# A memory-bound decode step on one core: from a planned tile program to one looped program per engine, with a running maximum

## The chip, the core and the metric

The kernel runs on one core of a Trainium2 chip. TensorE (PE) multiplies matrices, VectorE (DVE) and ScalarE (ACT) work on vectors, GpSimd (POOL) sets up a constant, and SyncE (SP) issues the transfers between the chip's main memory and the on-chip buffers; 16 DMA engines carry them out. Each engine follows its own instruction stream and waits for the others by semaphores. The metric is the device time of one execution in microseconds (us); lower is better.

## The reference

One token (batch 1, length 1, width 1024) goes through two branches that a gate mixes. Everything is float32.

```python
x = A_x                                             # (1, 1, 1024)
g = sigmoid((x * gate_w).sum(-1, keepdims=True))
# branch a: attention, 32 query heads, 4 key/value heads, 65536 cached positions, head width 128
q = (x @ wq) as 32 heads                            # wq 1024 x 4096; 8 query heads share a key/value head
p = softmax(q . k * 128 ** -0.5)                    # k_cache, v_cache: (1, 4, 65536, 128)
a = (p @ v) as one row @ wo                         # wo 4096 x 1024
# branch b: gated feed-forward on the one token, which is always the one routed
y = (silu(x @ w_gate) * (x @ w_up)) @ w_down        # 1024 x 3584, 1024 x 3584, 3584 x 1024
b = x + y * sigmoid(x @ w_r)
out = g * a + (1 - g) * b
```

The key and value caches are 134 MB each and the weights 78 MB; each is used once.

## The kernel before, in words

The arrays are laid out on the host so that every load is 128 rows, one for each partition, with up to 64 KB in a row. `stream` is a pool of two buffers of 64 KB a partition (`bufs=2`); `room` takes the next one, `load` fills it from SP's queue (line 70). All large loads share these two in turn: a load can be issued when PE has finished with the buffer two loads back. The order of the work is that of the program text, and the framework that it is written in places the waits.

For each of the four head groups (one key/value head and its eight query heads):

- `queries` multiplies x with the group's part of wq and spreads the eight queries into `qp` as stationary operands of 32 columns (L130, L138).
- Eight chunks of 8192 positions, two to a load of keys (8.39 MB). `score_chunk` does 16 products of 512 columns in four column groups of the array, which run beside each other (L149); in the profile each float32 product is two instructions. ACT copies the scores out of PSUM into a buffer of their own (L153), and DVE takes their row maximum (L154). The scores of all eight chunks are kept.
- `neg_max`, once per group: the maximum over all chunks and rows goes through a small product (L164) and becomes the exponential's bias `nb` (L169).
- Eight chunks again, two to a load of values: `value_chunk` exponentiates a chunk (L173), DVE transposes it in blocks of 32 (L175), and PE does 16 products that add into `acc` over all chunks (L178).
- `project` divides by the sums and multiplies with the group's part of wo into `att` (L191, L193, L201). wo of the group and wq of the next come in one load.

Into the key and value loops `load_eighth` (L237) puts 16 transfers of 64 KB: each brings eight rows of two of the 28 blocks of w_down, into a buffer `early` of their own. Four are issued in each head group, two between key loads and two between value loads:

```python
    eighths = [slice(32 * q + r, 32 * q + r + 29, 4) for r in range(4) for q in range(4)]

    def load_eighth():
        rows = eighths.pop()
        a = begins[w0 + b_early]
        nc.sync.dma_start(early[rows], tail[rows, a : a + 2 * D].rearrange("p (b n) -> p b n", b=2))
```

After the groups comes the tail. `load_rest` (L218) brings the last group's wo, then w_gate, w_up and w_down in pieces, through the same two buffers. `up_proj` makes the gate and up rows (L276), brings them into columns (L281, L284), and the product is `hp` (L295). The down-projection takes 4 products of 256 columns a block into `y` (L312); the last block is cut in two pieces of columns with loads of their own (L319). DVE joins y, att and x (L324), and SP stores the result (L325). At the end of the program the framework has all engines meet and clears the semaphores (L355).

Of the kernel before, what the change touches and what calls it, by code (L numbers as in the profile page):

```python
# [2 lines left out]

# [6 lines left out]
F32 = mybir.dt.float32  # L10
AF = mybir.ActivationFunctionType
ALU = mybir.AluOpType
# [7 lines left out]
SK = 65536  # L20
F = 3584
CH = 8192
NCH = SK // CH
NL = NCH // 2
NM = CH // 512
NB = CH // P
W = 16384
KB = D // P
NQ = D // 4
FB = F // P  # L30
FQ = FB // 4
SCALE = DH ** -0.5


@with_exitstack
def gated_mix_kernel(ctx: ExitStack, tc: tile.TileContext, x, vecs, k_t, v, wq0, wo_wq, tail, out):

    nc = tc.nc
    const = ctx.enter_context(tc.tile_pool(name="const", bufs=1))
    stream = ctx.enter_context(tc.tile_pool(name="stream", bufs=2))
    scores = ctx.enter_context(tc.tile_pool(name="scores", bufs=NCH + 2))
    work = ctx.enter_context(tc.tile_pool(name="work", bufs=2))
    ps_s = ctx.enter_context(tc.tile_pool(name="ps_s", bufs=2, space=bass.MemoryType.PSUM))
    ps_o = ctx.enter_context(tc.tile_pool(name="ps_o", bufs=2, space=bass.MemoryType.PSUM))
    ps_1 = ctx.enter_context(tc.tile_pool(name="ps_1", bufs=1, space=bass.MemoryType.PSUM))  # L60

    def room(*shape):
        t = stream.tile([P, W], F32, name="st", tag="st")
        names = " ".join("abcd"[: len(shape)])
        t = t[:, : math.prod(shape)]
        return t.rearrange(f"p ({names}) -> p {names}", **dict(zip("abcd", shape))) if len(shape) > 1 else t

    def load(src, *shape):
        t = room(*shape)
        nc.sync.dma_start(t, src)  # L70
        return t


    xk = const.tile([P, 3, KB], F32, name="xk")
    nc.scalar.dma_start(xk, vecs)
    x_row = const.tile([P, NQ], F32, name="x_row")
    nc.vector.memset(x_row, 0.0)

    wq_t = load(wq0, KB, HG * DH)

    ident = const.tile([P, P], F32, name="ident")
    make_identity(nc, ident)
    ones = const.tile([P, P], F32, name="ones")
    nc.vector.memset(ones, 1.0)

    sel = const.tile([P, 32], F32, name="sel")
    nc.vector.tensor_reduce(sel, ident.rearrange("p (j q) -> p q j", q=32), AX.X, ALU.add)
    sel8 = const.tile([P, HG], F32, name="sel8")
    nc.vector.tensor_reduce(sel8, ident.rearrange("p (a h) -> p h a", h=HG), AX.X, ALU.add)
    nsel = const.tile([P, HG], F32, name="nsel")  # L90
    nc.vector.tensor_scalar_mul(nsel, sel8, -SCALE)
    sel4 = const.tile([P, 4], F32, name="sel4")
    nc.vector.tensor_copy(sel4, ident.rearrange("p (j h) -> p j h", h=32)[:, :, 0])


    xp = const.tile([P, KB, 32], F32, name="xp")
    nc.vector.memset(xp, 0.0)
    nc.vector.tensor_copy(xp[:, :, 0], xk[:, 0, :])

    qp = const.tile([P, 2, 4, 32], F32, name="qp")  # L100
    nc.vector.memset(qp, 0.0)
    op = const.tile([P, HG, 32], F32, name="op")
    nc.vector.memset(op, 0.0)
    hp = const.tile([P, FB, 32], F32, name="hp")
    nc.vector.memset(hp, 0.0)


    dots = const.tile([P, 2, KB], F32, name="dots")
    for i in range(2):
        nc.vector.tensor_mul(dots[:, i, :], xk[:, 0, :], xk[:, 1 + i, :])  # L110
    dsum = const.tile([P, 2], F32, name="dsum")
    nc.vector.tensor_reduce(dsum, dots, AX.X, ALU.add)  # L112
    ps = ps_1.tile([P, P], F32, name="ps_m", tag="m")
    nc.tensor.matmul(ps[:, :2], ones, dsum, start=True, stop=True)  # L114
    sig = const.tile([P, 2], F32, name="sig")
    nc.scalar.activation(sig, ps[:, :2], AF.Exp, scale=-1.0)
    nc.vector.tensor_scalar_add(sig, sig, 1.0)
    nc.vector.reciprocal(sig, sig)
    gate = sig[:, 0:1]
    rest = const.tile([P, 2], F32, name="rest")  # L120

    nc.vector.tensor_scalar(rest[:, 0:1], gate, -1.0, 1.0, op0=ALU.mult, op1=ALU.add)
    nc.vector.tensor_mul(rest[:, 1:2], rest[:, 0:1], sig[:, 1:2])
    att = ps_1.tile([P, NQ], F32, name="att", tag="att")

    def queries(g, wq_t):
        ps = ps_s.tile([P, 512], F32, name="ps_q", tag="s")
        for k in range(KB):
            for j in range(4):
                nc.tensor.matmul(  # L130
                    ps[32 * j : 32 * j + 32, :NQ], xp[:, k, :], wq_t[:, k, j * NQ : (j + 1) * NQ],
                    start=(k == 0), stop=(k == KB - 1),
                )
        q_sb = work.tile([P, NQ], F32, name="q_sb")
        nc.vector.tensor_copy(q_sb, ps[:, :NQ])  # L135
        pt = ps_1.tile([P, P], F32, name="ps_m", tag="m")
        for e in range(2):
            nc.tensor.matmul(pt[:, 4 * e : 4 * e + 4], q_sb[:, e * DH : (e + 1) * DH], sel4, start=True, stop=True)  # L138
# [220 lines left out]
```

## Time and profile before

| what | value |
|---|---|
| median of 3 runs | 819.33 us (819.08 to 819.88) |
| span of the profiled execution, first to last instruction | 817.2 us |
| profiled execution's own device time | not given; the median is 2.1 us above the span |
| instructions | 6762, of them 3142 products and 3142 weight loads on PE |
| bytes moved | 346.47 MB, 424 GB/s over the span |
| mean granted TensorE clock | 0.730 |

An engine's share of busy time is an average; which work sets the end is read from the stretches and from the chain of waits. "PE" counts products and "PEld" weight loads, which run beside them. In the table by stretches each row has the stretch, its length, the busy time and the number of instructions of each engine, the granted clock of PE (1.00 is full), the busy share of the DMA engines (it can be a little over 1, as overlapping packets count twice) and the rate. In the chain a row is: start, length, what ran.

### The profile page before, as it was taken

The numbers are of one execution on the slowest core, as the hardware profiler recorded it, in microseconds if no ns is written. First come the engines' busy times: TensorE is split into PE (matmuls) and PEld (weight loads), VectorE is DVE, ScalarE is ACT, GpSimd is POOL, SyncE is SP. The second block draws the span as 40 slices with busy tenths as digits, with TensorE's granted clock in tenths as the row PEclk, the third lists the DMA queues.
The fourth block names the chain that finished last, engine by engine and source line by source line (L and its number), as shares of the span: only waits on it lengthen the run. The fifth ranks groups of instructions, "written<-read, shape, count | busy, mean of one in ns | idle before, by whom it ended". The sixth has DMA issues, their size and how long they took to land.

```text
span 817.2 us, 6762 instructions
## 1 busy us (share of the span) xinstructions
PE 396.5 (49%) x3142; PEld 129.6 (16%) x3142; DVE 64.4 (8%) x149; ACT 45.6 (6%) x101; POOL 0.7 (0%) x6
## 2 busy tenths in 40 slices
PE   2445454444444444454544555455444544444657
PEld 1111111112111111112111111122111111121214
DVE  2000020000000200000000200000000200000000
ACT  0000020000000200000000300000000300000000
POOL 0000000000000000000000000000000000000000
PEclk9667776776677667766677767777777677776768
DMA  9999999999999999999999999999999999999996
GB/s 411 411 456 415 420 453 420 434 430 440 424 427 427 420 433 432 433 434 431 423 427 427 427 430 440 427 440 424 421 433 424 433 427 442 424 403 438 413 412 268
DMA packets 7355, 346.47 MB, mean 424 GB/s; under 512 B 1048, under 2 KB 1184, under 8 KB 1440
## 3 DMA queue, kind: packets, MB, share of 16 engines
q1 hardware_dynamic: 7184, 346.04, 98.8%
q8 instruction: 24, 0.39, 0.2%
q10 hardware_dynamic: 144, 0.01, 0.0%
q14 instruction: 3, 0.02, 0.0%
HBM read 346.05 MB, written 0.00 MB: 423 GB/s over the span
## 4 chain that ended last, share of the span: by engine, by line
DMA 72%; PE 25%; ACT 1%; issue 0%; DVE 0%; SPq 0%; ACTq 0%
DMA st<-in_k_t 30%; DMA st<-in_v 26%; DMA st<-in_tail 10%; PE ps_s L149 9%; PE acc L178 9%; DMA st<-in_wo_wq 7%; PE att L201 2%; PE ps_f L276 2%; PE y L312 2%; PE ps_q L130 1%; ACT s L173 1%; PE ps_t L284 0%; ACT row L281 0%; PE y L319 0%; DVE mx L154 0%
## 5 line engine op out<-in xcount | busy, mean ns | idle before, releaser
L149 PE MATMUL ps_s<-st,qp 128*32 128x512 f32 x1024 | 145.6, 732 | 168.1 <-DMA st<-in_k_t 168.1
L178 PE MATMUL acc<-st,pt 128*32 128x512 f32 x1024 | 146.7, 737 | 126.1 <-DMA st<-in_v 126.1
L149 PEld LDWEIGHTS ps_s<-st,qp 128*32 128x32 f32 x1024 | 40.1, 131 | 270.3 <-issue 270.3
L178 PEld LDWEIGHTS acc<-st,pt 128*32 128x32 f32 x1024 | 37.7, 132 | 231.6 <-issue 188.1
L153 ACT ACTIVATE s<-ps_s 128x512 f32<-128x512 f32 x32 | 19.1, 597 | 575.0 <-PE ps_s L149 575.0
L276 PE MATMUL ps_f<-st,xp 128*32 128x448 f32 x256 | 34.6, 703 | 31.3 <-DMA st<-in_tail 31.3
L154 DVE TENSOR_REDUCE mx<-s 128x1 f32<-128x512 f32 x32 | 22.0, 686 | 295.7 <-ACT s L153 295.7
L201 PE MATMUL att<-st,op 128*32 128x256 f32 x256 | 25.2, 579 | 33.3 <-DMA st<-in_wo_wq 25.6
L175 DVE STREAM_TRANSPOSE pt<-s 128x512 f32<-128x512 f32 x32 | 22.7, 712 | 174.7 <-PE acc L178 170.9
L173 ACT ACTIVATE s<-s,nb 128x512 f32<-128x512 f32 x32 | 22.6, 707 | 10.7 <-DVE nb L169 10.7
L201 PEld LDWEIGHTS att<-st,op 128*32 128x32 f32 x256 | 13.1, 165 | 43.9 <-issue 43.3
L276 PEld LDWEIGHTS ps_f<-st,xp 128*32 128x32 f32 x256 | 9.4, 138 | 55.2 <-DMA st<-in_tail 34.5
L191 PE MATMUL ps_m<-sel,lb 128*128 128x8 f32 x8 | 2.3, 357 | 28.9 <-DVE lb L187 28.9
L130 PE MATMUL ps_q<-st,xp 128*32 128x256 f32 x256 | 16.2, 410 | 0.0
L312 PE MATMUL y<-st,hp 128*32 128x256 f32 x200 | 11.5, 392 | 0.0
L281 ACT ACTIVATE row<-ps_f 128x896 f32<-128x896 f32 x2 | 1.8, 917 | 151.6 <-PE ps_f L276 151.6
L130 PEld LDWEIGHTS ps_q<-st,xp 128*32 128x32 f32 x256 | 9.0, 118 | 6.2 <-issue 1.8
L189 DVE COPY o_sb<-acc 128x512 f32<-128x512 f32 x4 | 2.8, 692 | 90.6 <-PE acc L178 90.6
L114 PE MATMUL ps_m<-dsum,ones 128*128 128x2 f32 x2 | 0.6, 364 | 13.8 <-DVE dsum L112 13.8
L312 PEld LDWEIGHTS y<-st,hp 128*32 128x32 f32 x200 | 6.3, 115 | 5.4 <-issue 1.1
L191 PEld LDWEIGHTS ps_m<-sel,lb 128*128 128x128 f32 x8 | 2.0, 310 | 29.8 <-issue 29.8
L135 DVE COPY q_sb<-ps_q 128x256 f32<-128x256 f32 x4 | 1.7, 425 | 57.1 <-PE ps_q L130 57.1
(57 smaller groups left out, 51.3 us busy)
## 6 DMA issues: line engine op xcount, KB each, us to landing
st<-in_tail SPq DMA_DIRECT2D x3, 7168.0 KB, 25.1
st<-in_tail SPq DMA_DIRECT2D x2, 7680.0 KB
st<-in_wq SPq DMA_DIRECT2D x1, 4096.0 KB
st<-in_tail SPq DMA_DIRECT2D x1, 4096.0 KB
st<-in_tail SPq DMA_DIRECT2D x1, 2048.0 KB
st<-in_tail SPq DMA_DIRECT2D x2, 1024.0 KB
early<-in_tail SPq DMA_DIRECT2D x16, 64.0 KB
st<-in_tail SPq DMA_DIRECT2D x1, 512.0 KB
```

The costliest lines, as they stand in the source:

```text
L130: nc.tensor.matmul(ps[32 * j : 32 * j + 32, :NQ], xp[:, k, :], wq_t[:, k, j * NQ : (j + 1) * NQ], start=(k == 0), stop=(k == KB - 1),)
L149: nc.tensor.matmul(ps[32 * j : 32 * j + 32, :], qp[:, g % 2, s, :], kt[:, s, j, :], start=(s == 0), stop=(s == 3))
L153: nc.scalar.activation(t, ps, AF.Copy)
L154: nc.vector.tensor_reduce(mx[:, c : c + 1], t, AX.X, ALU.max)
L173: nc.scalar.activation(t, t, AF.Exp, bias=nb, scale=SCALE, accum_out=sums[:, c : c + 1])
L175: nc.vector.transpose(pt, t)
L178: nc.tensor.matmul(acc[32 * j : 32 * j + 32, :], pt[:, 32 * m : 32 * m + 32], vt[:, 4 * m : 4 * m + 4, :], start=(c == 0 and m < 4), stop= ...
L189: nc.vector.tensor_copy(o_sb, acc.rearrange("p (s d) -> p s d", s=4))
L191: nc.tensor.matmul(ps[:, :HG], lb, sel8, start=True, stop=True)
L201: nc.tensor.matmul(att[32 * j : 32 * j + 32, :], op[:, h, :], wo_t[:, h, j * NQ : (j + 1) * NQ], start=(g == 0 and h == 0), stop=(g == G - ...
L276: nc.tensor.matmul(ps[32 * j : 32 * j + 32, e, :n], xp[:, k, :], rest_of[first + k][:, at : at + n], start=(k == 0), stop=(k == KB - 1),)
L312: nc.tensor.matmul(y[32 * j : 32 * j + 32, :], hp[:, b, :], rest_of[w0 + b][:, j * NQ : (j + 1) * NQ], start=(b == order[0]), stop=False,)
```

## The change

The kernel is rewritten without the framework. Each engine has a program of its own with hand-written semaphore waits; PE's loops over groups and over block pairs are loops on the chip, and the other engines' programs are written out.

- There are three buffers of 64 KB a partition: `kb` for keys, `vb` for values, `wb` for weights. SP's queue alternates key and value loads. A key load waits until PE has done the scores of the key block before (`k_done`), a value load until PE has done the value products of the value block before (`v_done`). A weight load waits for the queries that use the other half of `wb` (`q_rows`).
- A block is one load, 16384 positions: 32 products into a PSUM tile S of 1024 columns. DVE takes the maximum straight from S; there is no copy to the on-chip buffer.
- The softmax keeps a running bound: after each key block the bound `nb` is updated, ACT exponentiates S at once, and DVE multiplies the running sums `l1` and `acc` with `alpha = exp(nd)` before it adds the new block. So scores and values of a block follow each other, 16 times in all.
- Output, gate and down products of 256 columns become products of 512; the sums of two column groups are joined at the end by a product with a selection matrix (`selj`). x @ wq, wo and w_down all run through `tiles`.
- The transfers of 64 KB are gone. x is loaded at the start from ACT's queue. In the tail the loads are: last wo, half of w_gate, half of w_gate, half of w_up, half of w_up, 16 blocks of w_down, then 8, 2, 1 and the last block in two pieces.
- There is no meeting of the engines at the end: SP waits for the store, and the program ends.

The core of the diff (removed lines stand in the kernel above):

```diff
+    def load(dst, src, sem, n=0):
+        if n:
+            sp.wait_ge(pe.sem, n)
+        sp.dma_start(dst, src).then_inc(sem, 16)
+
+    load(wb[:, W // 2 :], wq0, s_w)
+    for g in range(G):
+        for i in range(NL):
+            b = (g, i - 1) if i else (g - 1, NL - 1)
+            load(kb, k_t[g, i], s_k, k_done(*b) if b[0] >= 0 else 0)
+            load(vb, v_t[g, i], s_v, v_done(*b) if b[0] >= 0 else 0)
+        if g < G - 1:
+            load(wb, wo_wq[g], s_w, q_rows(g))
+        else:
+            load(wb[:, : W // 2], tail[:, : W // 2], s_w, q_rows(g))
...
+    for dst, n, sem, after in (
+        (kb, half, s_k, k_done(G - 1, NL - 1)),
+        (vb, half, s_v, v_done(G - 1, NL - 1)),
+        (wb, half, s_w, att_done(G - 1)),
+        (kb, half, s_k, FFN + 1),
+        (vb, W, s_v, FFN + 2),
+    ):
+        load(dst[:, :n], tail[:, at : at + n], sem, after)
+        at += n
+    parts = [8 * D, 2 * D, D] + [4 * (c1 - c0) for c0, c1 in PIECES]
+    for k, n in enumerate(parts):
+        to = at - down - W
+        load(wb[:, to : to + n], tail[:, at : at + n], s_part[k], 0 if k else FFN + 4)
+        at += n
...
+    with p.Fori(0, G):
...
+        with p.Fori(0, NL):
+            landed(s_k)
+            kv = kb.rearrange("p (c s j n) -> p c s j n", c=2, s=4, j=4)
+            for c in range(2):
+                for s in range(4):
+                    for j in range(4):
+                        ins = mm(
+                            S[32 * j : 32 * j + 32, 512 * c : 512 * c + 512], qp[:, 32 * s : 32 * s + 32], kv[:, c, s, j, :],
+                            s == 0, s == 3,
+                        )
+            pe(ins)
+            event()
+            pe(mm(M[:, :P], ones, md))
+            event()
+            landed(s_v)
+            vv = vb.rearrange("p (c m n) -> p c m n", c=2, n=512)
+            for c in range(2):
+                for m in range(16):
+                    j = m % 4
+                    ins = mm(
+                        A[32 * j : 32 * j + 32, :], pt[:, 512 * c + 32 * m : 512 * c + 32 * m + 32], vv[:, c, m, :],
+                        c == 0 and m < 4, c == 1 and m >= 12,
+                    )
+            pe(ins)
...
+        for i in range(NL):
+            dve.wait(pe, k_done(g, i))
+            d(v.tensor_reduce(m1, S, AX.X, ALU.max))
+            dve.own()
+            tell_pe(v.tensor_scalar_mul(md, ident, m1))
+            dve.wait(pe, m_done(g, i))
+            d(v.tensor_reduce(mh, M[:, :P].rearrange("p (a h) -> p h a", h=HG), AX.X, ALU.max))
+            dve.own()
+            d(v.tensor_mul(mh, mh, nsel))
+            dve.own()
+            d(v.tensor_reduce(nbi, mh, AX.X, ALU.add))
+            dve.own()
+            d(v.tensor_tensor(nb, nbi, nb0, ALU.min))
+            dve.own()
+            d(v.tensor_tensor(nd, nb, nb0, ALU.subtract))
+            dve.own()
+            d(v.tensor_copy(nb0, nb))
+            act.wait(dve)
+            act(a.activation(alpha, nd, AF.Exp))
+            act(a.activation(t, S, AF.Exp, bias=nb, scale=SCALE, accum_out=sums))
+            dve.wait(act)
+            d(v.scalar_tensor_tensor(l1, l1, alpha, sums, op0=ALU.mult, op1=ALU.add))
+            tell_pe(v.transpose(pt, t))
+            dve.wait(pe, v_done(g, i))
+            d(v.scalar_tensor_tensor(acc, acc, alpha, A, op0=ALU.mult, op1=ALU.add))
...
+    landed(s_v)
+    d1 = vb.rearrange("p (b n) -> p b n", n=D)
+    tiles(T, [hp[:, b, :] for b in range(16)], d1, False, False)
+    p.wait_ge(s_part[0], 16)
+    d2 = wb[:, : 8 * D].rearrange("p (b n) -> p b n", n=D)
+    join_ready = pe(tiles(T, [hp[:, 16 + b, :] for b in range(8)], d2, False, True))
+    later = wb[:, 8 * D : 11 * D].rearrange("p (b j n) -> p b j n", b=3, j=4)
+    for b in range(3):
+        if b != 1:
+            p.wait_ge(s_part[1 + b // 2], 16)
+        for j in range(4):
+            for (c0, c1), o in zip(PIECES, y):
+                mm(o[32 * j : 32 * j + 32, :], hp[:, JOIN + b, :], later[:, b, j, c0:c1], b == 0, False)
+        if b == 1:
+            event()
+            for j in range(4):
+                for (c0, c1), o in zip(PIECES, y):
+                    c = (j % 2) * 256
+                    mm(o[32 * j : 32 * j + 32, :], selj[:, j // 2, :], join[:, c + c0 : c + c1], False, False)
...
+    sp.wait_ge(dve.sem, dve.n)
+    sp.dma_start(out.rearrange("(j n) -> j n", j=4), fin[::32, :]).then_inc(s_out, 16)
+    sp.wait_ge(s_out, 16)
```

`event()` makes PE wait for one signal of `tell_pe`; `landed(sem)` makes it wait for a load; `pe(ins)` counts the steps that other engines wait for. `own()` makes DVE wait for its last step.

More of the change, by code (lines that the diff above doesn't have):

```diff
@@ L1 @@
[L1 to L5 removed]
+import concourse.bacc as bacc
 from concourse import mybir
[L7 to L8 removed]
 F32 = mybir.dt.float32
@@ new lines, in gated_mix, with tell_pe @@
+        pe(ins)
+        at += 4 * n
+    y_done = [pe.n - 1, pe.n]
+    pool(gp.memset(ident, 0.0))
+    pool.own()
+    pool(
+        gp.affine_select(
+            out=ident, in_=ident, compare_op=ALU.not_equal, fill=1.0, base=0, pattern=[[-1, P]], channel_multiplier=1
+        )
+    )
+    def tell_pe(ins):
+        ins.then_inc(to_pe, 1)
+    d = dve
+    d(v.memset(x_row, 0.0))
+    act.wait(dve)
+    a.dma_start(x_row[::32, :], x4).then_inc(s_x4, 16)
+    d(v.memset(join, 0.0))
+    d(v.memset(ones, 1.0))
@@ new lines, in gated_mix @@
+    d(v.tensor_copy(selj[:, :, 0], selq))
+    v.wait_ge(s_x, 16)
+    d(v.tensor_copy(xp[:, :, 0], xk[:, 0, :]))
+    for i in range(2):
+        d(v.tensor_mul(dots[:, i, :], xk[:, 0, :], xk[:, 1 + i, :]))
+    dve.own()
+    tell_pe(v.tensor_reduce(dsum, dots, AX.X, ALU.add))
+    act.wait(pe, 1)
+    act(a.activation(sig, M[:, :2], AF.Exp, scale=-1.0))
+    dve.wait(act)
+    d(v.tensor_scalar_add(sig, sig, 1.0))
+    dve.own()
+    d(v.reciprocal(sig, sig))
+    dve.own()
+    d(v.tensor_scalar(rest[:, 0:1], sig[:, 0:1], -1.0, 1.0, op0=ALU.mult, op1=ALU.add))
@@ new lines, in gated_mix @@
+    for u in range(2):
+        act.wait(pe, FFN + 3 * u + 2)
+        if u:
+            act.wait(dve)
+        a.activation(
+            row.rearrange("p (e n) -> p e n", e=2), R.rearrange("p (e n) -> p e n", e=2)[:, :, :FR], AF.Copy
+        ).then_inc(to_pe, 1)
+        cols = FFN + 3 * u + 3
+        if u == 0:
+            act.wait(pe, cols)
+            act(a.activation(hid, S[:, :FB], AF.Exp, scale=-1.0))
+            dve.wait(act)
+            d(v.tensor_scalar_add(hid, hid, 1.0))
+            dve.own()
+            d(v.reciprocal(hid, hid))
+            dve.own()
+            d(v.tensor_mul(hid, S[:, :FB], hid))
+            dve.own()
+            d(v.tensor_scalar_mul(hid, hid, rest[:, 1:2]))
+        else:
+            dve.own()
+            dve.wait(pe, cols)
+            tell_pe(
+                v.tensor_mul(
+                    hp[:, :, 0].rearrange("p (j m) -> p m j", j=4), S[:, :FB].rearrange("p (m j) -> p m j", j=4),
+                    hid.rearrange("p (m j) -> p m j", j=4),
+                )
+            )
```

448 lines of the change are left out of this document (185 added, 263 removed).

## The prediction

> **What bounds the kernel now.** I read the page from the top: busy times, the slices, the DMA queues.
>
> ```profile
> span 817.2 us, 6762 instructions
> PE 396.5 (49%) x3142; PEld 129.6 (16%) x3142; DVE 64.4 (8%) x149; ACT 45.6 (6%) x101; POOL 0.7 (0%) x6
> DMA  9999999999999999999999999999999999999996
> DMA packets 7355, 346.47 MB, mean 424 GB/s; under 512 B 1048, under 2 KB 1184, under 8 KB 1440
> q1 hardware_dynamic: 7184, 346.04, 98.8%
> q8 instruction: 24, 0.39, 0.2%
> ```
>
> No engine is over half busy; the 16 DMA engines are over 90% busy in all slices but the last. SP's queue (q1) moves 346.04 MB, and the new kernel must move the same weights and caches. So the question is only at what rate those bytes flow, and what lies ahead of the first and behind the last of them. Next I cut the span into stretches: per head group one from before the second key load lands to after the fourth (the key stretch) and one with the value loads and what follows (the value stretch); then the feed-forward tail.
>
> ```profile
> core 0: us, PE busy (x) PEld busy (x) DVE busy (x) ACT busy (x) POOL busy (x), PEclk, DMA share, GB/s
> 0.00:5.00 5.00, 0.00 (x0) 0.00 (x0) 2.03 (x6) 1.28 (x1) 0.70 (x6) 1.00 0.69 243
> 45.00:95.00 50.00, 20.38 (x140) 5.77 (x144) 2.75 (x4) 2.39 (x4) 0.00 (x0) 0.67 0.99 424
> 95.00:220.00 125.00, 65.44 (x520) 21.42 (x512) 11.13 (x26) 7.70 (x20) 0.00 (x0) 0.72 1.01 434
> 220.00:272.00 52.00, 20.53 (x144) 5.78 (x148) 3.43 (x5) 2.83 (x5) 0.00 (x0) 0.72 0.99 420
> 272.00:398.00 126.00, 65.74 (x516) 21.74 (x508) 11.13 (x26) 7.93 (x20) 0.00 (x0) 0.71 1.01 434
> 398.00:450.00 52.00, 19.86 (x144) 5.69 (x148) 3.43 (x5) 2.59 (x5) 0.00 (x0) 0.72 1.01 426
> 450.00:575.00 125.00, 64.43 (x516) 21.18 (x508) 11.83 (x27) 8.13 (x20) 0.00 (x0) 0.74 1.00 430
> 575.00:628.00 53.00, 22.26 (x148) 6.16 (x152) 2.74 (x4) 2.39 (x4) 0.00 (x0) 0.72 1.00 424
> 628.00:705.00 77.00, 34.88 (x252) 9.52 (x248) 8.56 (x17) 6.94 (x18) 0.00 (x0) 0.72 1.00 431
> 705.00:785.00 80.00, 45.52 (x370) 15.98 (x362) 1.77 (x6) 1.11 (x2) 0.00 (x0) 0.75 1.00 423
> 785.00:805.00 20.00, 12.30 (x114) 5.68 (x118) 0.21 (x1) 0.92 (x1) 0.00 (x0) 0.66 0.95 407
> 805.00:813.00 8.00, 8.00 (x155) 4.32 (x144) 0.84 (x2) 0.00 (x0) 0.00 (x0) 1.00 0.70 259
> ```
>
> The last column is what to read. The four value stretches (95, 272, 450, 628) have a weighted mean of 432.4 GB/s; I take it as the rate of an undisturbed queue. Against it the four key stretches lose (432.4-424)/432.4 x 50 = 1.0, then 1.5, 0.8 and 1.0 us: **4.3 us**. The feed-forward stretches lose 1.7 + 1.2 = **2.9 us**, the last eight microseconds **3.2 us**, the first five **2.2 us**. Check: 346.47 MB at 432.4 GB/s are 801.3 us, and with the 12.6 lost 813.9; the stream ends at about 813, where the last stretch was cut. So the stream explains the span, and about 10 us of it can be attacked.
>
> Last the chain, for how far ahead the loads are issued, and for the end.
>
> ```profile
> 32.46 9.95 PE ps_s L149 x64
> 42.43 30.30 DMA st<-in_k_t
> 72.86 8.53 PE ps_s L149 x64
> ...
> 634.02 0.70 DVE mx L154
> ...
> 634.94 0.30 DVE md L162
> ...
> 635.28 0.59 PE ps_m L164 x2
> ...
> 636.42 0.17 DVE nb L169
> ...
> 766.25 25.06 DMA st<-in_tail
> ...
> 799.98 13.23 PE y L312 x216
> ...
> 813.22 0.71 PE y L319 x16
> ...
> 813.95 0.48 DVE fin L324
> ```
>
> A load is issued when PE leaves the buffer before last (42.43) and lands 30.30 us later; its own 8.39 MB take 19.4 us at 432.4 GB/s, so 10.9 us of the load ahead were still to come: that is the margin before the queue runs dry.
>
> **The change, part by part.**
>
> *The buffers.* Two rotating buffers become three fixed ones (keys, values, weights), and key and value blocks alternate. The next key load waits for the scores of the key block before it, while one value load is in flight; the next value load waits for the value matmuls, while one key load is in flight. The margin is as now: PE needs 8.5 to 9.95 us of the 19.4 us that the other load takes, and 9.5 to 10.9 stay. At the ends of head groups it grows, since the weight buffer is free long before. I cost the new order at 0; its cover is that margin. If it goes, each block costs what is over.
>
> *The running maximum.* It puts the softmax between the scores and values of each pair, 16 times instead of four. The steps, with the chain's rows and these two:
>
> ```profile
> L175 DVE STREAM_TRANSPOSE pt<-s 128x512 f32<-128x512 f32 x32 | 22.7, 712 | 174.7 <-PE acc L178 170.9
> L173 ACT ACTIVATE s<-s,nb 128x512 f32<-128x512 f32 x32 | 22.6, 707 | 10.7 <-DVE nb L169 10.7
> ```
>
> Maximum over 1024 columns at most 2 x 0.70 = 1.4; from the product with the maximum to the negated bound 636.59 - 634.94 = 1.65; three more one-column DVE steps at 0.2 = 0.6; two exponentials, at most 0.2 + 2 x 0.71 = 1.6; one more DVE step 0.2; transpose at most 1.4; hops 0.3. Sum 7.2 us. Scores end 8.5 to 9.95 us after the key block has landed, so the transposed weights stand at 15.7 to 17.2, before the value block lands at 19.4. Hidden, with 2.2 us to spare, and behind that the 9.5 us margin of the queue. The value rescale (one DVE step over 128x512, about the 0.70 of a row above) lies beside the next load. Cost 0.
>
> *Removed: 16 small transfers* (load_eighth, 64 KB each, SP's queue). Both halves of a head group have two of them, yet only the key stretches lose rate. By the code the key ones fill rows 64 to 127 and the value ones rows 0 to 63; whether that is why is open, and so is whether the key stretches' loss is theirs at all. Bounds: 0 and 4.3. Beside them SP issues only the large loads in either kind of stretch, so I take 4.0. Their 1 MB does not vanish; it goes into the tail's loads at the same rate.
>
> The Trainium skill (DMA: Bandwidth & Descriptors, Measured) gives 0.95 us of DMA time for a 64 KB transfer. By that, estimated, 16 of them hold the queue for 15 us against 2.4 us for the same bytes in a large load, so 12.8 us would go, and the sum would be about 803.5. The value stretches, at full rate with half of these transfers in them, do not agree.
>
> *The start.* The 4 KB of x move from SP's queue in the tail to ACT's queue at the start, behind a DVE memset and the vecs load.
>
> ```profile
> xk<-in_vecs ACTq DMA_DIRECT2D x1, 12.0 KB, 12.4
> ```
>
> DVE waits for both before it copies the first queries, and PE for DVE. If x too lands 12.4 us after its issue, that is at about 14 us; the first scores start at 32.46, on the first key load. Covered by these 18 us, as are the four zeroing products that PE gets: 0.
>
> *The tail's loads* are issued farther ahead. Now the up-projection's load goes out at 766.25 and lands after 25.06 us, 18.2 of them its own 7.86 MB at 432.4: only 6.9 us ahead of it, issue latency included. The last three go out at the very end:
>
> ```profile
> SPq L218 <- PE y L312: 14.6, 1, 14.6
> 805.95 1.28 SPq L218 DMA_DIRECT2D st<-in_tail  x3
> ```
>
> In the new kernel the last five loads wait only for the first half of the up-projection, some 34 us before the end of the stream. Of the 2.9 us I take back 1.5 (bounds 0 and 2.9: loads of other row lengths follow one another there still), of the 3.2 us 0.8 (bounds 0 and 2.2; DMA engines that end at different times remain).
>
> *Code.* Loops replace 6284 PE instructions; q8's 0.39 MB are 0.9 us of stream. I take 0.4 back (bounds -0.3, if every iteration fetches anew, and 0.8).
>
> The stream thus ends 4.0 + 1.5 + 0.8 + 0.4 = **6.7 us** earlier (bounds about 0 and 10).
>
> *The end on PE.* The last 16 KB a row (2.1 MB, 4.9 us) come after the eight-block load (9.7 us), that after the sixteen-block one. With E the end of the stream, the sixteen blocks land at E-14.6 and cost 64 PE instructions of 512 columns, 8.5 to 9.95 us by the score rows: E-4.6 at the latest. The eight then cost, by
>
> ```profile
> L312 PE MATMUL y<-st,hp 128*32 128x256 f32 x200 | 11.5, 392 | 0.0
> ```
>
> 0.0575 us an instruction of 256 columns, 64 x 0.0575 = 3.7: E-0.9. Behind them stand three blocks, the join of the 512-wide sums and the last pieces, five sets of 16 short instructions. L319's set took 0.71 with its drain; I take 0.5 each and 0.2 once: E+1.8 (bounds E+1.0 and E+2.7). The copy of the sums for the join (0.7) runs beside the first two sets. Now PE ends at 813.93, E+0.9. So **+0.9 us**, less 0.1 because the last DVE step has 64 columns: **+0.8**.
>
> *The end barrier.*
>
> ```profile
> L355 SPq EVENT_SEMAPHORE  x7: 17/28/1067, 815.1 to 817.1; - x7
> ```
>
> SP's wait for the output ends at 815.1 + 1.07 = 816.2; the 1.0 us after it is barrier and clearing of semaphores. It goes: **-1.0**. The opening barrier belongs to the program's frame and I leave it.
>
> Sum: 817.2 - 6.7 + 0.8 - 1.0 = 810.3 us of span. The profiled execution's own time is not given; the median, 819.33, stands 2.1 above its span, and I keep that: **812.4 us**, 0.85% less.
>
> **The rivals.**
>
> *A. The loss of the key stretches is not the small transfers', and the tail keeps its gaps.* For it: the cause is read from a coincidence of stretches. Then only barrier, code and about 1 us of late issue go: 819.3 - 1.0 - 0.4 - 1.0 + 0.8 = **817.7 us**. Against it: four key stretches out of four, none of the value ones.
>
> *B. More is gained than costed*: the tail runs at the full rate (another 1.4), the engines end together (another 1.4), the code goes wholly (0.4), and something of the 2.1 us around the span goes with barriers and small transfers (up to 2): **807 to 809 us**. The 0.95 us a transfer of the Trainium skill (above) would be its far end. Against it: nothing in the new tail makes DMA engines wait for one another.
>
> *C. Slower: loop-backs drain the queue.* If PE, on jumping back, stands still for its code, the next scores or values start late. One fetch of 16 KB took 0.2% x 817.2 x 16 / 24 = 1.1 us by q8's row; the loop body is some 270 instructions, 17 KB, so two fetches, say twice 1.1 and twice a wait behind one 64 KB packet (65536 bytes at 1/16 of 432.4 GB/s, 2.4 us): 7 us. It decides from about 10 us on, when a value load's release comes after the key load ahead of it has landed; above that each microsecond costs 15 to 16. At 11 us: 812.4 + 15 = **827 us**. Against it: 7 is under 10, and the jump falls where PE waits for a load.
> The Trainium skill (Runtime: NRT & Kernel Launch, Instruction fetch mechanics) says that a taken branch out of the current window must fetch its target before execution goes on; no run here shows it yet, since the kernel before has no loop.
>
> *D. Slower: the clock in the tail.* PE waits before the sixteen-block load. If the granted clock stayed at half there, where the 805 to 813 row has 1.00, down-projection and join would take twice the full-clock time: (192 x 0.0575 + 2.7) x 2 = 27.5 us from E-14.6, ending at E+12.9 instead of E+1.8: about **823 us**. It decides from E+9. Against it: score bursts of 64 instructions after a wait took 9.95, not 14.7.
>
> **How the numbers follow.** Forecast 0.70, its own range 810 to 815 (about 2.5 us either way, from the bounds of the rate terms and of PE's end). A 0.13, B 0.10, C 0.04, D 0.03. 0.2%, about what a measurement can tell here from no change, is 1.6 us: the edge is 817.7, where A lies, and half of A counts as same, with a little of the forecast's upper side: faster 0.84, same 0.09, slower 0.07. The range 808.0 to 817.5 takes in the forecast, half of A and half of B; outside stay C, D, the other halves and the forecast's edges, about 0.2.
>
> **What would show it.** Right: the key stretches at 430 GB/s or more; last bytes at about 806; PE ending 1 to 3 us after the last landing; span's end within 0.2 us of the output's landing; no DMA slice under 9 but the last. Wrong, and how: key stretches still at 424 (A); value matmuls starting on the transposed weights and not on the value load's landing (the softmax is longer than 7.2 us); gaps in the stream at each jump back (C); a clock of 0.5 after the sixteen-block load (D).

## The result and the profile after

The changed kernel takes 806.84 us (median of four runs, 806.70 to 807.21) against 819.61 for the kernel before beside it (819.08 to 820.05): a ratio of 0.985, 95% interval 0.9836 to 0.9864. The gain is 12.8 us where 6.9 were forecast. The direction and the places were right; the size was not, and the time lies 1.2 us below the low end of the range.

The page of the changed kernel, its lines that answer to those shown of before:

```profile
span 805.3 us, 6266 instructions
PE 397.9 (49%) x2878; PEld 124.0 (15%) x2878; DVE 91.9 (11%) x243; ACT 24.2 (3%) x53; POOL 0.7 (0%) x6
DMA  9999999999999999999999999999999999999997
DMA packets 6935, 346.15 MB, mean 430 GB/s; under 512 B 904, under 2 KB 1040, under 8 KB 1296
q1 hardware_dynamic: 6776, 346.04, 99.3%
q8 instruction: 5, 0.08, 0.0%
```

SP's queue still moves 346.04 MB, and no engine is near to being the bound; DVE is busier by 27.5 us for the running maximum, at no cost to the kernel (the row of DVE further down). What moved is the rate, 424 to 430 GB/s over the span, and the last digit of the slices, 6 to 7. The line to keep in mind is the last: q8, the code, went from 24 packets to 5. The stream by stretches, in the columns of the prediction's table, and the last microseconds one by one:

```profile
core 0: us, PE busy (x) PEld busy (x) DVE busy (x) ACT busy (x) POOL busy (x), PEclk, DMA share, GB/s
45.00:95.00 50.00, 22.71 (x146) 6.31 (x150) 6.10 (x13) 1.95 (x5) 0.00 (x0) 0.67 1.01 439
95.00:220.00 125.00, 63.64 (x460) 19.59 (x452) 14.57 (x37) 2.59 (x6) 0.00 (x0) 0.75 0.99 429
220.00:272.00 52.00, 24.48 (x170) 7.05 (x174) 6.62 (x17) 2.59 (x6) 0.00 (x0) 0.71 1.02 441
272.00:398.00 126.00, 61.33 (x440) 18.78 (x431) 16.47 (x42) 3.89 (x9) 0.00 (x0) 0.74 1.00 434
5.00:705.00 700.00, 342.75 (x2402) 103.48 (x2406) 86.25 (x221) 20.91 (x49) 0.00 (x0) 0.74 1.00 435
705.00:785.00 80.00, 39.51 (x304) 14.44 (x296) 1.14 (x5) 2.03 (x3) 0.00 (x0) 0.69 0.99 429
799.00:800.00 1.00, 1.00 (x12) 0.26 (x8) 0.00 (x0) 0.00 (x0) 0.00 (x0) 1.00 0.97 380
800.00:801.00 1.00, 1.00 (x28) 0.63 (x24) 0.27 (x1) 0.00 (x0) 0.00 (x0) 1.00 0.41 154
801.00:802.00 1.00, 1.00 (x40) 0.89 (x32) 0.42 (x1) 0.00 (x0) 0.00 (x0) 1.00 0.11 39
```

The same view of the kernel before, the long stretch and its last microseconds:

```profile
5.00:705.00 700.00, 329.83 (x2498) 103.35 (x2502) 59.10 (x133) 42.27 (x97) 0.00 (x0) 0.72 1.00 430
809.00:810.00 1.00, 1.00 (x24) 0.54 (x20) 0.00 (x0) 0.00 (x0) 0.00 (x0) 1.00 0.98 372
810.00:811.00 1.00, 1.00 (x24) 0.60 (x20) 0.00 (x0) 0.00 (x0) 0.00 (x0) 1.00 0.55 208
811.00:812.00 1.00, 1.00 (x28) 0.52 (x21) 0.00 (x0) 0.00 (x0) 0.00 (x0) 1.00 0.24 92
812.00:813.00 1.00, 1.00 (x24) 0.44 (x16) 0.00 (x0) 0.00 (x0) 0.00 (x0) 1.00 0.12 44
```

Two things are to be seen. Over the 700 us of attention the queue runs at 435 against 430 GB/s: 5/430 x 700 = 8.1 us (give or take one and a half, since both rates are rounded). These rates count a packet whole where it starts, and sixteen packets of 64 KB are 1.05 MB, 21 GB/s of a stretch of 50 us. Spread over the time that they took, the packets of the two traces give 434.0 against 430.0 GB/s, 6.5 us. Key and value stretches are no more told apart, since the loads alternate; the 429 of one stretch and the 441 of the next belong to one steady stream, 433.9 to 434.3 when spread. And the stream now ends sharply. A DMA share of 0.55, then 0.24, then 0.12 means that fewer and fewer of the 16 DMA engines still have packets: they end apart. Before, these shares leave 0.02 + 0.45 + 0.76 + 0.88 = 2.1 us unused; after, up to the last bytes at 801.6, about 0.03 + 0.59 + 0.5 = 1.1.

The chain of waits after, its end:

```profile
787.43 13.23 PE T L140 x96
800.66 0.36 PE Y L140 x8
...
802.69 0.34 PE Y L140 x7
803.03 0.02 issue
803.05 0.49 DVE fin L381 x2
```

The last bytes come 11.4 us earlier than before (801.6 against 813.0; 6.7 were forecast), PE ends 1.4 us behind them, and the span ends with the landing of the output at 805.3.

### The profile page after: what moved, and what is told of

It reads as the page before. It is cut to its first block, busy times and chain, and to the rows that moved or that the text cites. A ratio compares the mean times of both kernels' runs of the same rounds, so it can differ in the third digit from the quotient of the medians.

```text
span 805.3 us, 6266 instructions
## 1 busy us (share of the span) xinstructions
PE 397.9 (49%) x2878; PEld 124.0 (15%) x2878; DVE 91.9 (11%) x243; ACT 24.2 (3%) x53; POOL 0.7 (0%) x6
## 3 DMA queue, kind: packets, MB, share of 16 engines
q1 hardware_dynamic: 6776, 346.04, 99.3%
## 5 line engine op out<-in xcount | busy, mean ns | idle before, releaser
L140 PE MATMUL S<-kbuf,qp 128*32 128x512 f32 x1024 | 146.0, 734 | 156.3 <-PEq L137 156.3
L140 PE MATMUL A<-vbuf,pt 128*32 128x512 f32 x1024 | 144.3, 727 | 129.3 <-PEq L137 129.3
L140 PEld LDWEIGHTS S<-kbuf,qp 128*32 128x32 f32 x1024 | 40.1, 132 | 259.0 <-issue 259.0
L140 PEld LDWEIGHTS A<-vbuf,pt 128*32 128x32 f32 x1024 | 39.9, 131 | 222.2 <-issue 222.2
L317 DVE TENSOR_REDUCE m<-S 128x1 f32<-128x1024 f32 x16 | 19.6, 1224 | 292.6 <-PE S L140 292.6
L140 PE MATMUL T<-wbuf,op 128*32 128x512 f32 x128 | 22.1, 854 | 26.0 <-PEq L137 26.0
L140 PE MATMUL R<-wbuf,xp 128*32 128x512 f32 (+1 forms) x192 | 23.7, 644 | 5.9 <-PEq L137 5.9
L140 PE MATMUL R<-kbuf,xp 128*32 128x448 f32 x128 | 16.4, 678 | 17.8 <-PEq L137 17.8
L337 DVE STREAM_TRANSPOSE pt<-t 128x1024 f32<-128x1024 f32 x16 | 19.8, 1237 | 0.0
L334 ACT ACTIVATE t<-S,nb 128x1024 f32<-128x1024 f32 x16 | 17.5, 1096 | 0.0
```

Of the source, the lines that this page charges most:

```text
L140: return p.matmul(o, w, r, start=first, stop=last)
L317: d(v.tensor_reduce(m1, S, AX.X, ALU.max))
L334: act(a.activation(t, S, AF.Exp, bias=nb, scale=SCALE, accum_out=sums))
L337: tell_pe(v.transpose(pt, t))
```

## The experiments

So 5.9 us of gain are not in the sum. Candidates: the small transfers cost more than the key stretches showed; the code costs more than its bytes; the tail's gap or the end costs more; or the new order of loads itself is faster. The runs undo one part of the change in the changed kernel, or do one part in the kernel before. Times are medians, each beside runs of the kernel before on the same chip (819.1 to 819.3); the last column is the difference from the changed kernel's 806.8.

| what | us | ratio to before, 95% | from after |
|---|---|---|---|
| before, one early 1 MB transfer | 813.15 | 0.9910 to 0.9937 | +6.3 |
| before, no small transfers, tail recut | 813.54 | 0.9917 to 0.9944 | +6.7 |
| after, small transfers back (mixed rows) | 814.04 | 0.9921 to 0.9948 | +7.2 |
| after, the same bytes over all rows | 809.90 | 0.9869 to 0.9900 | +3.1 |
| after, small transfers on rows 0 to 63 | 811.89 | 0.9895 to 0.9925 | +5.1 |
| after, small transfers on rows 64 to 127 | 817.44 | 0.9972 to 0.9991 | +10.6 |
| after, loops written out | 809.93 | 0.9870 to 0.9900 | +3.1 |
| after, tail loads issued later | 807.19 | 0.9836 to 0.9863 | +0.4 |
| after, one tail load issued too late | 809.88 | 0.9863 to 0.9894 | +3.0 |
| after, two meetings at the end | 808.15 | 0.9845 to 0.9875 | +1.3 |
| after, partition id read again | 806.99 | 0.9834 to 0.9861 | +0.2 |
| after, softmax 16 us longer | 849.49 | 1.0347 to 1.0379 | +42.7 |
| after, four parts undone together | 818.73 | 0.9983 to 1.0002 | +11.9 |
| the same and the late tail load | 821.17 | 1.0012 to 1.0031 | +14.3 |

An interval is about 1.2 us to either side; the runs of one kernel mostly agree within a microsecond. Differences under 0.5 are read as nothing.

**The small transfers.** First in the kernel before: one transfer of the same 1 MB over all 128 rows, in place of the sixteen of eight rows each.

```diff
     def load_eighth():
-        rows = eighths.pop()
+        if not eighths:
+            return
+        eighths.clear()
         a = begins[w0 + b_early]
-        nc.sync.dma_start(early[rows], tail[rows, a : a + 2 * D].rearrange("p (b n) -> p b n", b=2))
+        nc.sync.dma_start(early, tail[:, a : a + 2 * D].rearrange("p (b n) -> p b n", b=2))
```

> The kernel before, with the same two blocks of w_down brought by one transfer of 1 MB over all 128 rows (behind the second key load of the first head group) instead of 16 of 64 KB. Theory S (the small transfers slow the stream where they lie, and by loading some DMA engines more than others drive the engines apart, which costs the tail): the key stretches come to 433 GB/s, the last eight microseconds lose 1 us or less instead of 3; about 813 us. Theory C (code fetches drive the engines apart): only the 4 us of the key stretches return, 815.5 us, and the tail still loses its 5 us. Theory O (neither; the loss of the key stretches belongs to the key loads or their order): within 0.5 us of the kernel before.

Measured: 813.15 us, 6.2 less than the kernel before. The key stretches come up, by the stretches of this run:

```profile
core 0: us, PE busy (x) PEld busy (x) DVE busy (x) ACT busy (x) POOL busy (x), PEclk, DMA share, GB/s
45.00:95.00 50.00, 19.41 (x132) 5.42 (x136) 2.74 (x4) 2.39 (x4) 0.00 (x0) 0.67 1.02 439
220.00:272.00 52.00, 20.88 (x148) 5.77 (x148) 3.43 (x5) 2.99 (x5) 0.00 (x0) 0.72 1.00 434
5.00:705.00 700.00, 338.75 (x2546) 106.52 (x2550) 59.10 (x133) 42.27 (x97) 0.00 (x0) 0.72 1.00 433
705.00:785.00 80.00, 41.42 (x326) 14.48 (x322) 1.77 (x6) 1.11 (x2) 0.00 (x0) 0.71 0.97 418
```

424 and 420 became 439 and 434 (spread over their packets' time, 427.3 and 423.7 became 432.6 and 433.0): the loss of the key stretches is the small transfers', and rival A is out. From 430 to 433 GB/s over 700 us are 4.9 us.

Then the other way round, sixteen of them put back into the changed kernel between its loads. They fill a half of the weight buffer that is dead at that time, and nothing reads them, so they are 1.05 MB more, 2.4 us at 435 GB/s. Four forms: rows as in the kernel before; the same bytes as sixteen transfers of 128 rows by 512 bytes; only rows below 64; only rows from 64.

```diff
+    eighths = [slice(32 * q + r, 32 * q + r + 29, 4) for r in range(4) for q in range(4)]
+    def small():
+        rows = eighths.pop()
+        sp.dma_start(wb[rows, : 2 * D], tail[rows, a_e : a_e + 2 * D]).then_inc(s_e, 16)
...
             load(kb, k_t[g, i], s_k, k_done(*b) if b[0] >= 0 else 0)
+            if i in (1, 2):
+                small()
             load(vb, v_t[g, i], s_v, v_done(*b) if b[0] >= 0 else 0)
+            if i in (1, 2):
+                small()
+        sp.wait_ge(s_e, 64 * (g + 1))
```

The last line makes SP wait, before the weight load of each head group, until the small transfers so far have landed; it stands in all four forms. In the 128-row form the transfer is `sp.dma_start(wb[:, c : c + 128], tail[:, a_e + c : a_e + c + 128])`; in the last two, q runs over (0, 1) or (2, 3), twice.

> The changed kernel with 16 transfers of 64 KB (eight rows of 8 KB each, the rows in the same order as in the kernel before) put between its key and value loads; what they bring is not used, so 1.05 MB more are moved, 2.4 us at the stream's rate, and 809.3 us would be their bytes alone. Theory S: 4 us more where the rows from 64 on are filled and 2 to 4 us more at the end, as the engines end apart: 813 to 817 us. Theories C and O: 809.3 us.

> As the kernel with 16 unused transfers of 64 KB, but each over all 128 rows with 512 bytes in a row, so that all DMA engines get the same share; again 1.05 MB more are moved. If the unequal share is what costs (theory S): 809.5 us and engines that end together. If the number of transfers costs, whatever their shape: as the other, 813 us or more.

> The changed kernel with 16 unused transfers of 64 KB as in the earlier run, all of them to rows 0 to 63; 2.4 us for the bytes, that is 809.3 us. If the rows decide (rows from 64 on are filled across the ports of other engines): 809.5 to 811 us. If any eight-row transfer costs the same: 814 us as with mixed rows.

> The same with all of them to rows 64 to 127. If the rows decide: 817 to 819 us, twice the loss of the mixed rows. If any eight-row transfer costs the same: 814 us.

Measured: +7.2, so 4.8 beyond the bytes; +3.1 as even rows, 0.7 beyond them; +5.1 on low rows (2.7 beyond, a little more than was expected); +10.6 on high rows (8.2 beyond). So it is not the number of transfers: sixteen even ones cost next to nothing. It is not SP's wait either, which the even form has too. It is their shape, and high rows cost three times what low rows do. The long stretch of the low-row and then of the high-row run:

```profile
5.00:705.00 700.00, 341.61 (x2376) 102.20 (x2376) 84.65 (x216) 20.91 (x49) 0.00 (x0) 0.73 1.00 434
```

```profile
5.00:705.00 700.00, 335.53 (x2336) 100.66 (x2340) 84.64 (x216) 20.93 (x49) 0.00 (x0) 0.73 1.00 431
```

The prediction's guess from the code, rows from 64 on, holds for the rate, and the packet records of the two traces say more. Each of these transfers is eight packets of 8 KB on eight of the 16 DMA engines, 0.31 us each. Followed by their times, the packets of all sixteen transfers of the low-row run fall to the same eight engines as far as these can be told apart, so those are 16 x 0.31 = 4.9 us behind at the end: that is the +5.1, bytes included, and the rate over 700 us hardly shows it (434). Beside a high-row transfer, in addition, 16 to 24 of the 64 KB packets under way take 2.5 to 2.8 us instead of 2.42; beside the low-row ones, but for the first, at most one does. Why high rows slow the others stays open.

**The code.** PE's loops written out, as the kernel before has them:

```diff
-    with p.Fori(0, G):
+    for _ in range(G):
...
-        with p.Fori(0, NL):
+        for _ in range(NL):
```

> The changed kernel with PE's loops written out, so that PE again fetches some 0.3 to 0.4 MB of code instead of 0.08. Theory C: 0.7 us for the bytes, and the engines end 4 to 6 us apart, the stream's last stretch loses 2 to 3 us more: 809 to 810 us. Theory S: the bytes alone, 807.5 us, with the engines still ending within 2 us of each other.

Measured: +3.1 us. The queue of the code and the last microseconds of this run:

```profile
q8 instruction: 23, 0.38, 0.2%
```

```profile
core 0: us, PE busy (x) PEld busy (x) DVE busy (x) ACT busy (x) POOL busy (x), PEclk, DMA share, GB/s
799.00:800.00 1.00, 1.00 (x12) 0.14 (x4) 0.00 (x0) 0.00 (x0) 0.00 (x0) 1.00 0.92 375
800.00:801.00 1.00, 0.93 (x12) 0.29 (x12) 0.00 (x0) 0.00 (x0) 0.00 (x0) 1.00 0.66 269
801.00:802.00 1.00, 1.00 (x16) 0.38 (x12) 0.00 (x0) 0.00 (x0) 0.00 (x0) 1.00 0.56 229
802.00:803.00 1.00, 1.00 (x16) 0.27 (x9) 0.00 (x0) 0.00 (x0) 0.00 (x0) 1.00 0.50 201
803.00:804.00 1.00, 1.00 (x21) 0.52 (x17) 0.16 (x1) 0.00 (x0) 0.00 (x0) 1.00 0.38 154
804.00:805.00 1.00, 1.00 (x36) 0.89 (x32) 0.54 (x1) 0.00 (x0) 0.00 (x0) 1.00 0.17 61
```

The added code is 0.30 MB, 0.7 us of stream. The rest shows at the end: for five microseconds part of the DMA engines are through and the others are not, and up to the last bytes at 804.7 these rows leave 0.08 + 0.34 + 0.44 + 0.50 + 0.62 + 0.53 = 2.5 us unused, against 1.1. A code packet is 16 KB on one DMA engine. The loads give every engine the same share (followed by their times, the 64 KB packets are 288 on each of the 16), and engines that are through stay idle while others have packets left. By the packet records the engines end 4.7 us apart here and 1.8 in the changed kernel. That the late ones are those that carried more code is inferred, since the records do not name the engine; the ends stand in steps (seven near 800.3, then 802.1, 803.0 and 804.3 to 804.7) of about the time of a fetch and what it delays. For a fetch takes 0.93 us in this run, where 16 KB of a load take 0.61 in the kernel before, and the 64 KB packet that starts as it ends takes 2.92 instead of 2.42. Over 16 engines that is 18 x (0.32 + 0.50) / 16 = 0.9 us, and 0.7 + 1.4 + 0.9 = 3.0 of the 3.1 us are shown so.

**The tail.** In the kernel before, the small transfers were taken out and the tail recut so that its loads fit two buffers, to close the gap that the run with one early transfer has at 760. By the chain of that run a load goes out there and lands after 21.58 us, 18.1 of them its own 7.86 MB, so that little was left ahead of it:

```profile
763.29 21.58 DMA st<-in_tail
```

```diff
-    gps = up_proj(1, {3: 7, 7: 11})
+    gps = up_proj(1, {3: 6, 6: 9})
...
-    ups = up_proj(1 + KB, {11: 15, 15: 25})
+    ups = up_proj(1 + KB, {9: 13, 13: 19})
...
-    load_rest(w0 + 8, w0 + 16, w0 + 20, w0 + 22, w0 + 24)
+    load_rest(w0 + 2, w0 + 18)
```

> The kernel before without small transfers and with the tail's loads cut anew within its two buffers: the three gate pieces end with a load of their own, so that no load has to wait for products on both sides of the gate's epilogue, and w_down comes as two blocks, then sixteen, then the last twelve cut in six. In the run with one early transfer the stream stood still for some 1.9 us around 760. If that gap is a load issued too late behind the epilogue: 811.2 us, and no slice of the tail under 9 but the last. If it comes from drifted engines alone: 813 us as there.

Measured: 813.54, not better than 813.15. The chain of this run:

```profile
705.04 21.02 DMA st<-in_tail
...
763.50 30.97 DMA st<-in_tail
```

The late issue moved from 763 to 705 instead of going away, so this run tells nothing of its price. Two runs in the changed kernel do: tail loads issued only when the buffer before last is through (the products of the sixteen blocks are counted in twelve and four for this), and one load held back until the queue is empty.

```diff
-        (wb, half, s_w, att_done(G - 1)),
-        (kb, half, s_k, FFN + 1),
-        (vb, W, s_v, FFN + 2),
+        (wb, half, s_w, FFN + 1),
+        (kb, half, s_k, FFN + 2),
+        (vb, W, s_v, FFN + 4),
...
-        load(wb[:, to : to + n], tail[:, at : at + n], s_part[k], 0 if k else FFN + 4)
+        load(wb[:, to : to + n], tail[:, at : at + n], s_part[k], (FFN + 5, 0, FFN + 7, 0, 0)[k])
```

> The changed kernel with the tail's loads issued as late as a ring of two buffers would let them: each waits for the products of the load two before it, the last three for twelve of the sixteen blocks. Theory L (late issue by itself cost the kernel before some 2.3 us in the tail): 809 us. Theory D (late issue costs only where the DMA engines have drifted apart, since then the foremost run dry before the load is issued; here they run together): 807.2 us or less.

```diff
+        if n == W:
+            sp.wait_ge(s_gap, 1)
         load(dst[:, :n], tail[:, at : at + n], sem, after)
```

> The changed kernel with the load of the sixteen blocks of w_down held back by six transposes behind the first half of the up-projection, so that it goes out at about 767, as late against the end of the load before it as in the kernel before (766.25 there, with the stream running thin from 766 to 772). If a load that late costs the stream some 1 to 2 us even with the engines together: 808 to 809 us. If it costs nothing: 806.8 us.

The semaphore is set by DVE, behind six extra transposes that wait for the first half of the up-projection.

Measured: +0.4 for the later issue. The DMA issues of that run show what was left ahead of a load:

```profile
wbuf<-in_tail SPq DMA_DIRECT2D x1, 7168.0 KB, 24.7
```

Of the 24.7 us to its landing 16.9 are its own (7.34 MB at 435 GB/s), so 7.8 of other loads were still to come. The load held back costs +3.0. Its issue, and the stretch around it:

```profile
768.08 0.33 SPq L104 DMA_DIRECT2D vbuf<-in_tail  x1
```

```profile
765.00:772.00 7.00, 3.75 (x22) 1.17 (x26) 2.98 (x3) 0.00 (x0) 0.00 (x0) 0.50 0.53 183
```

Half of seven microseconds is idle, 0.47 x 7 = 3.3 us (2.6 by the packets' own times), and the whole kernel is 3.0 us later: here the time in which the queue is empty is lost one for one, and lateness that leaves it filled costs nothing that can be told from no change.

**The end and the start.** Two meetings of all engines behind the store, `nc.all_engine_barrier()` twice, and apart from that the partition id read at the start again (`enable_partition_id=False` left out).

> The changed kernel with two meetings of all engines at its end, behind the store. By the trace of the kernel before they cost 1.0 us: 807.8 us. If the gap between span and device time (2.1 us before, 1.4 now) also hangs on them: 808.5 us. If nothing waits for them: 806.8 us.

> The changed kernel with the number of the core handed to the program again, which the change leaves out of the program's frame. If the 0.6 us between span and device time are its work: 807.4 us, with the same span. Otherwise 806.8 us.

Measured: +1.3 us and +0.2; between the two, which share a chip, 1.2. In the profiled executions the span of the first grows from 805.3 to 806.5, and the time around it from 1.4 us to 1.8. The partition id is nothing.

**The order and the softmax.** Thirteen more transposes of 1.24 us, one behind the other, between a block's scores and its values: 16.1 us more.

```diff
+            for _ in range(13):
+                dve.own()
+                d(v.transpose(pt, t))
+            dve.own()
             tell_pe(v.transpose(pt, t))
```

> The changed kernel with the softmax step lengthened by 13 transposes of 1.24 us, 16.1 us a block. The step takes 6.2 us now and the transposed weights wait 4.5 us for the values. If the stream's margin is the only cover, as the prediction's sum over margins had it (2 us to the landing, 9.5 us of queue): about 16.1 - 14 = 2 to 4 us a block, 35 to 65 us more. If the serial loop decides (scores 8.5, softmax 22.3, values 9.1, together about 40 us a block against 38.8 of the stream): about 1 to 1.5 us a block, 15 to 25 us more. If more than that is hidden: 807 us.

Measured: +42.7 us, 2.7 a block. PE's line of time in this run (start, length, what, and in brackets the idle time before it):

```profile
301.26 7.07 PE L140 MATMUL S<-kbuf,qp 128*32 128x512 f32 x64 [3.51 <-PEq L137]
331.65 9.59 PE L140 MATMUL A<-vbuf,pt 128*32 128x512 f32 x64 [21.10 <-PEq L137]
341.50 4.07 PE L140 MATMUL S<-kbuf,qp 128*32 128x512 f32 x36 [0.27 <-PEq L137]
```

From one block's scores to the next are 40.2 us, where two loads take 2 x 19.3 = 38.6 at 435 GB/s. The cover of the softmax is real and has an end: of 16.1 added microseconds a block about 13.4 were paid for by slack, near the 4.5 us of spare that the block of after shows (below) and the 9.5 of the queue. Which of the two limits named ahead of the run decides is not settled: in this block PE goes from scores to values to the next scores with 0.27 us of idle time, so its own chain of work sets the 40.2; in other blocks it waits 1.4 to 3.5 us for the keys, and from one block to the next are up to 42.6.

**All together.** Small transfers, written-out loops, later tail loads and two meetings, all in one; then with the late load too.

> The changed kernel with all of it undone at once: 16 unused transfers of 64 KB, PE's loops written out, the tail's loads issued late, two meetings at the end. 1.05 MB more are moved than in the kernel before, 2.4 us. If these parts are the whole gain: 819.6 + 2.4 = 822 us. If they simply add up (7.2 + 3.1 + 1.0 and nothing for the late issue): 818 us. If there is another part, such as the order of the key and value loads: 815 us or less.

> The kernel with all parts undone at once (818.7 us, of which 2.4 are the unused bytes), with this late load on top. If the late load is what was still missing of the kernel before's 819.1: 820.5 to 821.5 us. If something else is missing: 819 us or less.

Measured: +11.9, where the four alone give 7.2 + 3.1 + 0.4 + 1.3 = 12.0: they add up. Its time outside the span is 819.5 - 817.4 = 2.1 us, against 1.8 in every run of the kernel before beside it. Less the 2.4 us of added bytes it stands at 816.3; 2.8 us to the 819.1 beside it are missing. With the late load it is 818.8 net against 819.3, but that closes nothing: by the packet records its engines are idle for 4.4 us between 760 and 780, those of the kernel before for 0.3.

The packet records, added up over each trace and divided by 16 engines, show where the missing part lies. "At full pace" is what the bytes would take if all moved as a usual 64 KB packet of the changed kernel does (2.418 us); "slower packets" is what the packets took beyond that; "idle" is engine time without a packet, 1.8 us of it at the start in every run.

| kernel, us | last bytes | at full pace | slower packets | idle |
|---|---|---|---|---|
| before | 813.0 | 799.0 | 9.9 | 4.2 |
| before, one early 1 MB transfer | 807.5 | 799.0 | 4.8 | 3.8 |
| after | 801.6 | 798.2 | 1.4 | 2.1 |
| after, small transfers on rows 0 to 63 | 807.0 | 800.7 | 1.7 | 4.7 |
| after, small transfers on rows 64 to 127 | 811.4 | 800.7 | 6.3 | 4.4 |
| after, loops written out | 804.7 | 798.9 | 2.5 | 3.4 |
| after, four parts undone together | 813.0 | 801.3 | 6.8 | 4.9 |

The kernel before has 3.1 us more in slower packets than the kernel with four parts undone, and 0.7 less idle: about the 2.8. In the stretch from 705 to 785 alone it moves 421.1 GB/s, when spread, against 431.5 there and 433.6 after, 1.9 of 2.3 us; and all along its 64 KB packets take 2.421 us where those after take 2.418, 0.8 us over the 280 of an engine. No run has put the old tail or the old order of loads into the changed kernel, so why these packets are slower stays open, and up to these 3 us could be due to the new loads and their order.

## Why the prediction was right or wrong

The plan of the sum was right: this kernel is its stream of 346 MB, and the change gains by what disturbs that stream. By its steps:

- *The undisturbed rate, 432.4 GB/s: too low.* The changed kernel runs 700 us at 435 (434.0 when spread). The two small transfers in each value stretch are not the reason: without them, with one early transfer, the value stretches move 432.2 to 432.6, when spread, as before. The code fetches are a part of it (433.3 over 700 us with loops written out), the slightly longer packets of the kernel before (2.421 against 2.418 us) are most of the rest. Everything measured against 432.4 came out too small.
- *Small transfers, 4.0 us (bounds 0 and 4.3): right cause, too small.* 4.8 in the changed kernel, 6.2 in the one before. The loss of the key stretches was there. The step went wrong in reading a value stretch at full rate as one in which the transfers cost nothing: on low rows they leave the rate as it is and put eight engines behind, which is paid at the end (2.6 us of idle time for sixteen in the changed kernel). In the kernel before the gain shows as slower packets (9.9 against 4.8 us), hardly as idle time: with the engines together, its late load leaves them idle for 1.4 us between 760 and 780, against 0.3.
The Trainium skill (DMA: Bandwidth & Descriptors, Measured) gives 0.95 us of DMA time for a transfer of 64 KB, measured over 128 partitions and issued from GpSimd. Here one issued from SP cost, its bytes included, 7.2 / 16 = 0.45 us with mixed rows, 0.66 on high rows and 3.1 / 16 = 0.19 as 128 rows: that time for a single transfer is not what a transfer in a filled queue costs, and the estimate of 803.5 that followed from it is not borne out.
- *Code, 0.4 us (bounds -0.3 and 0.8): the step that failed most.* It measured 3.1. The step counted the bytes of the code as a share of the stream, 0.7 of the 3.1, and not that each fetch sets one DMA engine back, by more than its bytes' time. The 1.4 us by which engines end apart stood in rival B as a thing that nothing in the new tail removes; the loops removed it.
- *The tail's loads, 1.5 (0 to 2.9) and 0.8 (0 to 2.2).* Issuing farther ahead is worth 0.4 where the queue stays filled; what counts is a gap, 3.0 where a hole of about 3 was made. The old tail did lose 2.3 us between 705 and 785 against the new one, within the bounds, but only 0.7 of that is idle engines; the rest is slower packets, for a reason that stays open. Less idle time at the very end comes with the code (1.4 us).
- *Order of the buffers and softmax, 0: right.* The rows of DVE and the idle times in brackets below show the softmax of a block and its cover:

```profile
284.78 8.49 PE L140 MATMUL S<-kbuf,qp 128*32 128x512 f32 x64 [9.71 <-PEq L137]
293.34 1.22 DVE L317 TENSOR_REDUCE m<-S 128x1 f32<-128x1024 f32 x1 [17.45 <-PE S L140]
...
298.29 1.24 DVE L337 STREAM_TRANSPOSE pt<-t 128x1024 f32<-128x1024 f32 x1
...
304.06 9.09 PE L140 MATMUL A<-vbuf,pt 128*32 128x512 f32 x64 [8.57 <-PEq L137]
```

From 293.3 to 299.5 are 6.2 us (at most 7.2 by the sum), and PE starts the values at 304.06, 4.5 us later: it waits for the load, not for the weights.
- *The end on PE: right.* The sixteen-block load's products start at E-14.2 (forecast E-14.6), the eight blocks end at E-0.9 (the same), the five sets take 2.4 us, and the end is E+1.4 (E+1.8, bounds 1.0 and 2.7).
- *The end barrier, 1.0 of span: right, with 0.3 more around it.* The meetings put back 1.2 to 1.3 us. The 2.1 us around the span, kept in the sum, compared a median with the span of another execution: in all runs of the kernel before beside the experiments device time stands 1.8 us above the span of the same execution. It became 1.4, and the 0.4 come back with the two meetings.

Of the rivals, A is refuted by the first run. D needed the clock to stay at half. Its sign did show, for five to six microseconds behind the sixteen-block load:

```profile
787.40:790.00 2.60, 2.57 (x13) 0.72 (x17) 0.00 (x0) 0.00 (x0) 0.00 (x0) 0.50 0.93 403
793.00:796.00 3.00, 3.00 (x32) 0.95 (x28) 0.00 (x0) 0.00 (x0) 0.00 (x0) 1.00 0.82 350
```

Then the clock is 1.00 to the end, and the 64 instructions took 9.75 us, within the 8.5 to 9.95 of the sum; D is refuted by that. C, the jumps that fetch code anew, is refuted by q8: five fetches in all, and no gap at a jump. The Trainium skill (Runtime: NRT & Kernel Launch, Instruction fetch mechanics) speaks of a stall after a taken branch whose target is not in the current window, and of full unrolling as what kernels prefer for that reason; in this kernel the loops are 3.1 us faster than the same instructions written out. B, more is gained than costed, comes nearest with its 807 to 809, by all four of its items: a tail at nearly the full rate (433.6 when spread), engines that end nearer together, the code, and the time around the span. Of the signs named, all that were to show the forecast right came as named, but the last bytes at 801.6 instead of about 806; of those that were to show it wrong, only the clock's, for a time.

## What to carry to other kernels

When a kernel is a stream, take its undisturbed rate from a run without the suspects, not from the stretches that look best, and do not take a stretch at full rate for one in which everything is free; price a small transfer or a code fetch not by its bytes but by the DMA engines it loads unevenly, which is read from the DMA share in the last microseconds. Loops on the chip pay here through the DMA queue, not through the engine that loops. A late issue was worth mending only where the queue ran empty; with 7.8 us of loads ahead it cost at most 0.4 us.

## What was not expected of the hardware

- Sixteen transfers of eight rows by 8 KB cost 8.2 us beyond their bytes when they go to rows from 64 on, 2.7 to rows below 64, and 0.7 as 128 rows by 512 bytes.
- Eighteen fetches of 16 KB, 0.09% of the bytes, made the kernel 3.1 us (0.4%) longer, nearly half of it at the end of the stream.
- Two meetings of the engines at the end cost 1.2 us of span and 0.4 outside it in the profiled executions, 1.2 to 1.3 by the medians.
